# Attention's softmax: the reciprocals of the row sums taken on GpSimd as a power, where VectorE's reciprocal took them

## The chip, the cores and the metric

The kernel runs on one core of a Trainium2 chip. The metric is the time of one execution on the device in microseconds (us), the median of the runs shown. The engines are named as in the profile: PE is TensorE (matrix products; PEld its weight loads), DVE is VectorE, ACT is ScalarE, POOL is GpSimd, SP is SyncE, which here issues the DMAs. Each engine works through its own queue in program order and waits on the others through semaphores.

## What the kernel computes

Sparse attention over 4 batches, 8 heads, 576 positions, 64 features per head, and behind it two dense layers. Only the attention is touched by the change; the rest is cut to one line each.

```python
scores = scale * np.matmul(q, k.transpose(0, 1, 3, 2))
...
mask_local = (rel >= 0) & (rel < stride)
mask_strided = (rel >= 0) & (pos[None, :] % stride == pos[:, None] % stride)
...
scores = scores - np.max(scores, axis=-1, keepdims=True)
attn = np.exp(scores)
attn = attn / (np.sum(attn, axis=-1, keepdims=True) + 1e-09)
return np.matmul(attn, v).astype(np.float32)
...
h = x @ w_in;  x = (h * np.cos(h)) @ w_out          # first layer, 512 -> 2048 -> 512
...
g = x @ w_gate;  return (silu(g) * (x @ w_val)) @ w_out   # second layer, 512 -> 1536 -> 512
```

The first four heads use the local mask (32 keys back), the last four the strided one (each 32nd key).

## The kernel before

The attention stage works on pairs of heads. A unit is one batch and one pair; the 16 units are taken two at a time, a strided one and a local one, and each is cut into three groups (`gs`, line 780). That makes 48 groups, a strided one (tiles `e_s`, `qks`, `pts`) and a local one (`e_l`, `qkl`, `pt`) in turn. A group holds three or four small softmax tiles side by side, 128 rows by 3x96 or 4x54 scores.

The order is written out by hand in one loop (line 816). Step k of it does one part of each of several groups, so that every part of a group lies some steps behind the one before it (`LAGS = (2, 5, 6, 7)`): the scores and the row maxima of group k, the exponentials of group k-1, the sums and the division of group k-2, the transposes of group k-5, the product with the values of group k-6, and the copy out of group k-7.

Who does what for a group: PE makes the scores (L464, L466, L467), the transposes (L499, L503) and the products with v (L521). DVE takes the maxima (`top`, L472) and the sums with the reciprocals (`sums`, L488, and `norm`, L491). POOL scales the maxima (L473) and multiplies the exponentials by the reciprocals (L493, in place in `e_s` or `e_l`). ACT makes the exponentials (L479) and empties PSUM (L510, L534, L543). The sums lie in a small tile `ls`, 128 rows by 3 or 4, of which there are five.

Between these parts the same loop hands out work for the weights of the layers that follow (`pump`, line 854): ACT reads raw weights (L252) and rounds them (L273), DVE takes their maxima (L255, L202), shifts and joins their bits (L259, L263) and makes the remainders (L276). In a step this filling stands in DVE's queue behind the sums and the maxima, and ahead of the reciprocals, since `norm` is called after `pump`.

Behind the attention come the first dense layer (L579 to L581 with L612 to L627), and the second one, which makes up most of the time.

Of the kernel before, what the change touches and what calls it, by code (L numbers as in the profile page):

```python
# [10 lines left out]
F32 = mybir.dt.float32  # L11
# [4 lines left out]
ALU = mybir.AluOpType  # L16
# [65 lines left out]
def build(tc, qk_l, qk_s, v_l, v_s, w_in, w_out, w_gate, w_val, w_out2, fixed, out):  # L82
    nc = tc.nc
    wide = w_in.dtype != F32
    with ExitStack() as ctx:
# [317 lines left out]
        ap = attn.enter_context(tc.tile_pool(name="attn", bufs=2, side="right"))  # L403
# [7 lines left out]
        e_l = [ap.tile([128, 3, LW + 1], F32, name=f"e_l{i}", bufs=1) for i in range(4)]  # L411
        hot = ap.tile([128, 512], BF16, name="hot", bufs=1)
        nc.vector.memset(hot, 1.0)
        v_pair = [ap.tile([128, 2 * SP, 128], F32, name=f"v_pair{i}", bufs=1) for i in range(2)]
        for d in e_s:
            nc.gpsimd.memset(d, 0.0)
# [29 lines left out]
        class Group:  # L446
# [41 lines left out]
                nc.vector.tensor_reduce(out=self.l, in_=self.e[..., 0:self.w + 1], op=ALU.add, axis=AX.X)  # L488

            def norm(self):  # L490
                nc.vector.reciprocal(out=self.l, in_=self.l)  # L491
                e = self.e[..., 0:self.w]
                nc.gpsimd.tensor_tensor(out=e, in0=e, in1=self.l.unsqueeze(len(e.shape) - 1).to_broadcast(list(e.shape)), op=ALU.mult)  # L493

# [875 lines left out]
```

## Time and profile before

| what | us |
|---|---|
| median of three runs | 852.34 |
| lowest and highest of them | 852.09, 852.67 |
| the profiled execution, its own time | 853.48 |
| its span, from the first instruction to the last | 851.7 |
| PE busy in the span | 842.2 |
| DVE busy | 649.6 |
| ACT busy | 519.3 |
| POOL busy | 199.6 |

The span is the part of the profiled execution that the trace shows; 1.8 us of its time lie around it. Busy times are averages over stages with different limits. The attention stage is the first 100 us or so of the span.

### The profile page before, as it was taken

How to read it: one execution, taken by the hardware profiler on the slowest of the kernel's cores; microseconds unless marked ns; L12 is line 12 of the kernel's file. 1: busy time of each engine (PE TensorE's matmuls, PEld its weight loads, DVE VectorE, ACT ScalarE, POOL GpSimd, SP SyncE). 2: the span in 40 equal slices, each digit the busy share in tenths (PEclk: the TensorE clock that was granted, in tenths of full speed). 3: DMA queues.
4: the chain of work that ended last, by engine and by line, in shares of the span. 5: the costliest groups of instructions: out<-in, count | busy, mean ns of one | idle time of the engine just before them, and what ended most of it. 6: DMA issues, size and time to landing. Idle time of an engine off the chain costs nothing.

```text
span 851.7 us, 18335 instructions
## 1 busy us (share of the span) xinstructions
PE 842.2 (99%) x7228; PEld 601.5 (71%) x7228; DVE 649.6 (76%) x1242; ACT 519.3 (61%) x1047; POOL 199.6 (23%) x281
## 2 busy tenths in 40 slices
PE   8999999999999999999999999999999999999998
PEld 5777544444444444566666888888888899999998
DVE  6999988997889878799996388567756765765562
ACT  6899989554656766778885466545445454444440
POOL 3554234111445546422223001000000000000000
PEclk9999999999999999999999999999999999999999
DMA  9998822897557566415356257767767688788894
GB/s 367 408 373 288 275 74 99 291 337 262 184 196 237 198 210 214 170 42 188 115 214 238 78 185 284 253 220 260 237 246 261 222 284 290 278 310 312 318 329 149
DMA packets 53622, 202.23 MB, mean 237 GB/s; under 512 B 5280, under 2 KB 15904, under 8 KB 49696
## 3 DMA queue, kind: packets, MB, share of 16 engines
q1 hardware_dynamic: 53536, 201.06, 66.5%
q8 instruction: 57, 0.93, 0.4%
q14 instruction: 29, 0.24, 0.1%
HBM read 177.05 MB, written 23.99 MB: 236 GB/s over the span
## 4 chain that ended last, share of the span: by engine, by line
PE 84%; DVE 7%; ACT 4%; DMA 2%; issue 1%; POOL 1%; SPq 0%; ACTq 0%; POOLq 0%
PE acc L733 13%; PE bank L579 12%; PE bank L581 12%; PE bank L580 12%; PE acc L581 7%; PE acc L579 7%; PE acc L580 7%; PE bank L464 3%; PE po L521 3%; DMA raw<-w_val 2%; POOL arena L627 1%; PE tp L499 1%; PE bank L466 1%; DVE pw_two L202 1%; PE bank L733 1%
## 5 line engine op out<-in xcount | busy, mean ns | idle before, releaser
L579 PE MATMUL bank<-xs,wi 128*128 128x256 f16 (+3 forms) x780 | 232.6, 298 | 0.8 <-DVE arena L1231 0.7
L581 PE MATMUL bank<-xs,wi 128*128 128x256 f16 (+3 forms) x780 | 232.6, 298 | 0.0
L580 PE MATMUL bank<-xs,wi 128*128 128x256 f16 (+3 forms) x780 | 232.6, 298 | 0.0
L627 POOL TENSOR_TENSOR arena<-tb,arena 128x512 f16<-128x512 f32 (+1 forms) x80 | 89.8, 1123 | 236.1 <-ACT arena L626 197.2
L581 PE MATMUL acc<-arena 128*128 128x512 f16 (+1 forms) x320 | 114.5, 358 | 1.4 <-DVE arena L276 1.4
L579 PE MATMUL acc<-arena 128*128 128x512 f16 (+1 forms) x320 | 114.5, 358 | 0.0
L580 PE MATMUL acc<-arena 128*128 128x512 f16 (+1 forms) x320 | 114.5, 358 | 0.0
L580 PEld LDWEIGHTS <-wi 128*128 128x128 f16 x880 | 86.1, 98 | 35.7 <-issue 1.2
L581 PEld LDWEIGHTS <-wi 128*128 128x128 f16 x880 | 86.1, 98 | 34.8
L579 PEld LDWEIGHTS <-wi 128*128 128x128 f16 x880 | 86.1, 98 | 34.7
L733 PEld LDWEIGHTS <-arena 128*128 128x128 f16 x1080 | 100.7, 98 | 8.2
L717 POOL TENSOR_TENSOR wi<-tb 128x256 f32<-128x256 f32 (+1 forms) x30 | 20.2, 674 | 337.4 <-DVE tb L699 337.4
L1231 DVE TENSOR_TENSOR arena<-bank,cv 128x512 f32<-128x512 f32 (+1 forms) x60 | 37.9, 636 | 66.0 <-PE bank L581 66.0
L702 ACT ACTIVATE arena<-tb 128x256 f16<-128x256 f32 (+3 forms) x59 | 28.7, 486 | 97.0 <-DVE tb L699 88.5
L581 PEld LDWEIGHTS <-arena 128*128 128x128 f16 x600 | 58.7, 98 | 34.6 <-DVE arena L276 1.9
L580 PEld LDWEIGHTS <-arena 128*128 128x128 f16 x600 | 58.7, 98 | 32.5
L579 PEld LDWEIGHTS <-arena 128*128 128x128 f16 x600 | 58.7, 98 | 32.4
L733 PE MATMUL acc<-arena 128*128 128x256 f16 (+1 forms) x684 | 80.2, 266 | 0.0
L626 ACT ACTIVATE arena<-tb 128x512 f16<-128x512 f32 (+1 forms) x80 | 46.6, 583 | 53.1 <-PE acc L581 51.6
L612 ACT ACTIVATE tb<-bank,quarter,c 128x512 int32<-128x512 f32 (+1 forms) x75 | 54.5, 726 | 27.3 <-PE bank L581 18.9
L699 DVE SCALAR_TENSOR_TENSOR tb<-tb,c,arena 128x512 f32<-128x512 f32 (+1 forms) x60 | 41.7, 695 | 34.5 <-ACT tb L694 34.4
L1227 ACT ACTIVATE cv<-bank 128x512 f32<-128x512 f32 (+1 forms) x90 | 49.3, 548 | 29.6 <-PE bank L581 28.6
(147 smaller groups left out, 1713.4 us busy)
## 6 DMA issues: line engine op xcount, KB each, us to landing
wi<-w SPq DMA_DIRECT2D x20, 1792.0 KB, 7.4
arena<-w SPq DMA_DIRECT2D x60, 576.0 KB, 4.9
raw<-w_out SPq DMA_DIRECT2D x56, 512.0 KB, 4.9
arena<-w SPq DMA_DIRECT2D x10, 1792.0 KB, 8.5
raw<-w_gate SPq DMA_DIRECT2D x24, 512.0 KB, 4.3
raw<-w_val SPq DMA_DIRECT2D x24, 512.0 KB, 5.6
w<-arena SPq DMA_DIRECT2D x42, 256.0 KB, 3.3
raw<-w_in SPq DMA_DIRECT2D x16, 512.0 KB, 9.1
```

The source lines that it names most:

```text
L464: nc.tensor.matmul(out=self.sc[r, i, :], lhsT=qk_t[self.i][r, q0:q0 + 64], rhs=qk_t[self.i][r, k0:k0 + w], start=i == 0, stop=False)
L579: nc.tensor.matmul(out=o, lhsT=w[:, 0, c], rhs=x[0], start=first, stop=False, **kw)
L580: nc.tensor.matmul(out=o, lhsT=w[:, 0, c], rhs=x[1], start=False, stop=False, **kw)
L581: nc.tensor.matmul(out=o, lhsT=w[:, 1, c], rhs=x[0], start=False, stop=last, **kw)
L612: nc.scalar.activation(out=c["w"].bitcast(I32), in_=c["ph"], func=AF.Identity, scale=turn[c["blk"]], bias=quarter)
L626: nc.scalar.activation(out=g[:, 0, 0:n], in_=w, func=AF.Copy)
L627: nc.gpsimd.tensor_tensor(out=g[:, 1, 0:n], in0=w, in1=g[:, 0, 0:n], op=ALU.subtract)
L699: nc.vector.scalar_tensor_tensor(out=t, in0=t, scalar=s_g[c["blk"]], in1=c["C"][m][:, 1, 0:c["n"]], op0=ALU.mult, op1=ALU.mult)
L702: nc.scalar.activation(out=to, in_=src, func=AF.Copy, scale=2.0 ** -11)
L733: nc.tensor.matmul(out=o[:, c], lhsT=w[:, 256 * i + 128 * c:256 * i + 128 * c + 128], rhs=unit(u)[:, x:x + h], start=j == i == 0 and c == ...
L1227: nc.scalar.activation(out=t, in_=src, func=AF.Copy)
L1231: nc.vector.tensor_tensor(out=c["C"][m][:, :, h * right:h * right + h], in0=p, in1=t, op=ALU.add)
```

## The change

A tile `minus` of 128 by 4 is filled with -1 once, at the start, by DVE. In `norm`, DVE's reciprocal of `ls` goes, and POOL raises each sum to the power of the matching element of `minus`, in place in `ls`; the multiplication of the exponentials by `ls` follows it on POOL as before. For a strided group of three tiles the power now covers three columns, where the reciprocal covered all four.

```diff
         hot = ap.tile([128, 512], BF16, name="hot", bufs=1)
         nc.vector.memset(hot, 1.0)
+        minus = ap.tile([128, 4], F32, name="minus", bufs=1)
+        nc.vector.memset(minus, -1.0)
...
             def norm(self):
-                nc.vector.reciprocal(out=self.l, in_=self.l)
+                l = self.ls[:, 0:self.n]
+                nc.gpsimd.tensor_tensor(out=l, in0=l, in1=minus[:, 0:self.n], op=ALU.pow)
                 e = self.e[..., 0:self.w]
                 nc.gpsimd.tensor_tensor(out=e, in0=e, in1=self.l.unsqueeze(len(e.shape) - 1).to_broadcast(list(e.shape)), op=ALU.mult)
```

POOL's queue at the first groups of the stage (`mx` are the maxima, `ls` the sums, `e_s_98` and `e_l_102` the exponentials of the first strided and local group), before:

```order
L473 TENSOR_SCALAR mx<-mx 128x4
L493 TENSOR_TENSOR e_s_98<-e_s_98,ls 128x2x2x54
L473 TENSOR_SCALAR mx<-mx 128x3
L493 TENSOR_TENSOR e_l_102<-e_l_102,ls 128x3x96
L473 TENSOR_SCALAR mx<-mx 128x3
```

and of the change, where lines 473 and 493 have become 475 and 496:

```order
L475 TENSOR_SCALAR mx<-mx 128x4
L494 TENSOR_TENSOR ls<-ls,minus 128x4
L496 TENSOR_TENSOR e_s_98<-e_s_98,ls 128x2x2x54
L475 TENSOR_SCALAR mx<-mx 128x3
L494 TENSOR_TENSOR ls<-ls,minus 128x3
L496 TENSOR_TENSOR e_l_102<-e_l_102,ls 128x3x96
L475 TENSOR_SCALAR mx<-mx 128x3
```

Each step now has one instruction more on POOL, between the scaling of the maxima of group k and the multiplication of group k-2. The multiplication waits for POOL's own power where it waited for DVE.

DVE's queue at two steps in the middle of the stage (`wi` and `raw` are the weights of the filling), before:

```order
L259 TENSOR_SCALAR wi<-wi 128x512
L491 RECIPROCAL ls<-ls 128x4
L488 TENSOR_REDUCE ls<-e_l_102 128x3
L472 TENSOR_REDUCE mx<-bank 128x3
L263 SCALAR_TENSOR_TENSOR wi<-raw,wi 128x512
L255 TENSOR_REDUCE pw_in<-raw 128x1
L491 RECIPROCAL ls<-ls 128x3
L488 TENSOR_REDUCE ls<-e_s_99 128x4
```

and of the change, with 488 now 490 and 472 now 474:

```order
L259 TENSOR_SCALAR wi<-wi 128x512
L490 TENSOR_REDUCE ls<-e_l_102 128x3
L474 TENSOR_REDUCE mx<-bank 128x3
L263 SCALAR_TENSOR_TENSOR wi<-raw,wi 128x512
L255 TENSOR_REDUCE pw_in<-raw 128x1
L490 TENSOR_REDUCE ls<-e_s_99 128x4
```

The reciprocals, which stood behind the filling of their step, are gone, and nothing else of DVE's order has moved. PE, ACT and SP keep their orders.

## Rows read from the trace of the kernel before

**Rows 1.** The page: the span, and busy time, share and instructions of engines.
```profile
span 851.7 us, 18335 instructions
PE 842.2 (99%) x7228; PEld 601.5 (71%) x7228; DVE 649.6 (76%) x1242; ACT 519.3 (61%) x1047; POOL 199.6 (23%) x281
```

**Rows 2.** Busy time in stretches (start:end, length, busy by engine, clock, DMA, GB/s).
```profile
20.00:90.00 70.00, 70.00 (x1173) 50.34 (x1171) 66.95 (x192) 65.50 (x249) 35.43 (x76) 1.00 0.93 350
...
200.00:220.00 20.00, 18.26 (x88) 8.14 (x87) 14.09 (x31) 9.57 (x16) 3.48 (x3) 1.00 0.41 155
```

**Rows 3.** The chain that ended last (start, length, work): scores of three-tile strided groups.
```profile
20.50 0.49 PE bank L464 x12
...
31.65 0.49 PE bank L464 x12
...
87.44 0.49 PE bank L464 x12
```

**Rows 4.** PE's waits from 10 to 110 us, all of them.
```profile
PE po L521 <- ACT pt L510: 0.3, 1, 0.3
```

**Rows 5.** POOL's groups by shape: count, busy us, mean ns, idle before and releasers.
```profile
L493 POOL TENSOR_TENSOR e_l<-e_l,ls 128x288 f32<-128x288 f32 x24 | 16.0, 667 | 17.7 <-DVE ls L491 12.5 <-ACT xy L534 2.3 <-ACT pt L510 2.1
L493 POOL TENSOR_TENSOR e_s<-e_s,ls 128x216 f32<-128x216 f32 x24 | 13.2, 549 | 19.2 <-DVE ls L491 8.6 <-ACT pts L510 3.7 <-PE bank L467 2.3
...
L473 POOL TENSOR_SCALAR mx<-mx 128x3 f32<-128x3 f32 x32 | 10.0, 311 | 5.1 <-DVE ls L491 2.2 <-DVE mx L472 1.7
...
L473 POOL TENSOR_SCALAR mx<-mx 128x4 f32<-128x4 f32 x16 | 5.4, 336 | 8.0 <-DVE mx L472 7.0 <-DVE ls L491 0.9
...
L417 POOL MEMSET e_s<- 128x4 f32 x4 | 0.4, 102 | 0.2
```

**Rows 6.** Line 491's instructions: ns min/median/max, first and last start.
```profile
L491 DVE RECIPROCAL ls<-ls x48: 159/167/172, 10.1 to 95.4; 128x4 f32<-128x4 f32 x24, 128x3 f32<-128x3 f32 x24
```

**Rows 7.** Timeline of DVE, start and length, from 7.0 and from 41.9 us.
```profile
7.83 0.38 DVE L472 TENSOR_REDUCE mx<-bank 128x4 f32<-128x216 f32 x1 [3.01 <-PE bank L467]
...
41.99 0.17 DVE L491 RECIPROCAL ls<-ls 128x4 f32<-128x4 f32 x1
42.08 0.42 DVE L488 TENSOR_REDUCE ls<-e_l 128x3 f32<-128x291 f32 x1
42.42 0.45 DVE L472 TENSOR_REDUCE mx<-bank 128x3 f32<-128x288 f32 x1
42.79 0.68 DVE L263 SCALAR_TENSOR_TENSOR wi<-raw,wi 128x512 int32<-128x512 int32 x1
```

**Rows 8.** Timeline of POOL from 41.0 us, and ACT's next exponentials.
```profile
41.24 0.19 POOL L473 TENSOR_SCALAR mx<-mx 128x4 f32<-128x4 f32 x1 [0.32 <-DVE mx L472]
42.34 0.55 POOL L493 TENSOR_TENSOR e_s<-e_s,ls 128x216 f32<-128x216 f32 x1 [0.91 <-PE po L521]
42.96 0.56 POOL L473 TENSOR_SCALAR mx<-mx 128x3 f32<-128x3 f32 x1
...
42.77 0.94 ACT L479 ACTIVATE e_s<-bank,mx 128x54 f32<-128x54 f32 x4
```

**Rows 9.** Timeline of POOL at the start: a memset that waits for POOL's own.
```profile
0.90 0.31 POOL L416 MEMSET e_s<- 128x256 f32 x1
1.27 0.10 POOL L417 MEMSET e_s<- 128x4 f32 x1
```

**Rows 10.** Lines 259, 263 and 276 until 100 us: ns min/median/max, first and last start.
```profile
L259 DVE TENSOR_SCALAR wi<-wi x16: 409/418/679, 18.6 to 74.0; 128x512 int32<-128x512 int32 x16
...
L263 DVE SCALAR_TENSOR_TENSOR wi<-raw,wi x16: 679/692/889, 19.0 to 74.7; 128x512 int32<-128x512 int32 x16
...
L276 DVE SCALAR_TENSOR_TENSOR wi<-wi,s x11: 735/751/1175, 79.2 to 99.6; 128x512 f16<-128x512 f32 x11
```

**Rows 11.** Timeline of POOL and DVE at 125 us, behind the attention stage.
```profile
125.42 1.16 POOL L627 TENSOR_TENSOR arena<-tb,arena 128x512 f16<-128x512 f32 x1 [1.78 <-ACT arena L626]
...
125.79 1.33 DVE L263 SCALAR_TENSOR_TENSOR cv<-raw,cv 128x512 int32<-128x512 int32 x1
```

## The prediction

> **What bounds the kernel now.** I read the page first: PE is busy for 842.2 of 851.7 us, DVE for 649.6, POOL for only 199.6 [rows 1]. The shares of the whole say little about a change that touches the first 100 us, so the next view was the busy time of the stretch from 20 to 90 us, the steady part of the attention stage. There PE is busy for all 70 us, DVE for 66.95, ACT for 65.50 and POOL for 35.43 [rows 2]. Three engines are nearly full and the fourth is half full.
>
> Which of the three sets the pace shows in the chain of waits and in PE's own waits. In the chain the stage is PE's work end to end. The scores of a strided group of three tiles (0.49 us) come round once in six steps, at 20.50, 31.65 and so on to 87.44: seven of them, with six intervals of 11.15 or 11.16 us in the mean [rows 3]. A step lasts 11.15 / 6 = 1.858 us, and it does so whatever the filling in it is. From 10 to 110 us PE has a single wait, of 0.3 us [rows 4]. So PE paces the stage by its own instructions; DVE and ACT fit under it with 4 to 6 per cent to spare, and the reader should not take DVE's 96 per cent for the bound.
>
> POOL's 50 per cent are one scaling of the maxima and one multiplication in each step. Over 48 steps the scalings take 10.0 + 5.4 = 15.4 us and the multiplications 16.0 + 13.2 = 29.2 us [rows 5], together 0.93 us in a step. So POOL has 1.86 - 0.93 = 0.93 us free in a step. The rows put most of that idle time down to waiting for the reciprocal, line 491 [rows 5].
>
> **What is removed.** 48 reciprocals of 0.167 us leave DVE [rows 6]. What one holds up there is less: the sums behind it start 42.08 - 41.99 = 0.09 us after it [rows 7], so DVE's queue is lighter by 48 x 0.09 = 4.3 us. I count this as nothing, because PE paces these steps and does not wait for DVE. The multiplication's wait for DVE goes too. A reciprocal stands behind the filling of its step, while the sums stand before it; the power can start when the sums and the scaling of the next maxima are done, in the row at 41.24 + 0.19 = 41.43, where the multiplication starts at 42.34 [rows 8]. These 0.9 us are the same free time seen from the other side, and the power spends it.
>
> **What is added on DVE.** One memset of 128 by 4. POOL's memset of that size took 0.10 us [rows 5]; DVE sits idle for 3.01 us before the first maxima [rows 7], which covers it. Without that cover it would cost 0.1 us.
>
> **What is added on POOL.** 48 powers, and a wait of the multiplication for its own engine. The wait has a row: the memset at 1.27 waits for the one that ends at 0.90 + 0.31 = 1.21, so 0.06 us [rows 9].
>
> No row shows a power. From below, the nearest row is the scaling of the maxima, of the same engine and size, 0.19 us where nothing delays it [rows 8]; it does two multiplications. A memset of the size takes 0.102 us [rows 5], so reading and two arithmetic operations on four columns cost 0.09 us over the bare instruction. A power needs a logarithm, a product and an exponential. I take six such pairs of operations beyond the scaling, 0.19 + 6 x 0.093 = 0.75 us; as the upper bound I take fifteen, 0.19 + 15 x 0.093 = 1.6 us. The low end is 0.19 us itself. Six and fifteen are chosen, not read; it is the weakest point of the working. A mean of 0.75 us lies nearer to the scaling than to the multiplication of 512 columns by line 627, 1.16 us [rows 11].
>
> **How much of the free time the power can use.** Not all 0.93 us. The scaling takes 0.19 us alone, but 15.4 / 48 = 0.32 us in the mean [rows 5]: the one at 42.96 lasts 0.56 us and ends with DVE's L263, which runs from 42.79 to 43.47 [rows 7, 8]. It stands just where DVE begins its filling. The multiplication escapes this today, since it starts behind the filling (its reciprocal is last there). With the change both the power and the multiplication follow the scaling at once, in the middle of the filling. I give each of them the scaling's mean delay, 0.32 - 0.195 = 0.125 us, 0.25 together. What is left for the power is 0.93 - 0.06 - 0.25 = 0.62 us.
>
> **The sum.** Power 0.75 less 0.62 is 0.13 us a step by which POOL, not PE, then paces the stage; over 48 steps 6.2 us. What is late next: POOL's scaling of the maxima, which stands in the same queue behind the multiplication, with the exponentials waiting for it. From its end at 41.43 to the exponentials at 42.77 there are 1.3 us of reserve [rows 8], used up in the first ten steps; after that ACT, then the banks of the scores and the transposes on PE, wait in turn. I let this reserve stand against the longer first steps. I count on nothing behind the stage to give it back. Against the profiled execution that is 853.48 + 6.2 = 859.7 us; that execution lies 1.1 us above the median of 852.34, and the runs' median is what is forecast: 858.5 us.
>
> **The rules beside it.** That DVE and POOL hold each other up is a row: L263 at 125.79 takes 1.33 us beside a POOL multiplication that runs from 125.42 to 126.58, and its median is 0.69 [rows 10, 11]. The Trainium skill, "SBUF — State Buffer", section "SBUF: two separate sides", says that DVE instructions with two SBUF inputs or in a two-port mode share a port pair with GpSimd under an exclusive lock held for the whole instruction. By that rule the trace agrees, and the longer POOL's power is, the longer DVE is shut out; the third rival below is what this would do. The Trainium skill, "GPSIMD Engine Reference", section 4.1, advises VectorE for elementwise work and calls GpSimd about twice as slow with two inputs. By that factor alone the power would take an estimated 2 x 0.167 = 0.33 us, and the sum would be no change; no run here shows that the factor holds for a power, which is no simple operation.
>
> **The rivals.**
>
> *The power is cheap: no change.* It decides from 0.62 us downward. Then POOL's free time covers it, PE goes on pacing the stage at 1.858 us a step, and the time stays at 852.3 us (851 to 854). For it speaks that the scaling with its two operations costs only 0.19 us; against it that a power is many operations.
>
> *The power is dear: much slower.* Above the upper bound, if the engine takes it in a slow form. Each us beyond 0.62 costs 48 us: at 1.6 us 899, at 2.6 us 947.
>
> *DVE becomes the bound.* DVE has 70 - 66.95 = 3.05 us free in 70 [rows 2], 0.08 us a step, and gains 0.09. In the stage it has 16 + 16 + 11 = 43 instructions of the kind that POOL shuts out [rows 10], 0.9 a step. If each meets the power and the multiplication (0.75 + 0.61) and waits half of them, that is 0.9 x 0.68 = 0.61 us, 0.44 more than is free, and over 48 steps 21 us: 873 us. Against it: instructions that wait for each other also spread out, and not each meets one.
>
> *DVE's relief pays: faster.* DVE holds the path later, and the one stretch where PE then loses time is 200 to 220 us, 20 - 18.26 = 1.74 us [rows 2]. If the 4.3 us of relief arrived there, the time would be 850.6. Against it: PE ends the attention stage when it did, and the program ties DVE's order to PE's.
>
> **How the numbers follow.** The forecast, POOL pacing the stage with a power of 0.62 to 1.6 us, gets 0.42; the cheap power 0.34; the dear one 0.14; DVE as the bound 0.05; the relief 0.05. The forecast's own range is 853 to 899. The range to hold it 8 times in 10 runs from 850.5 (the relief) to 890 (a power of 1.4 us), and leaves out the dear power and the upper end of the forecast. About 0.2 per cent (1.7 us) is what a measurement of this kernel can tell from no change. Faster: 0.05, the relief. Same: 0.34 and 0.02 of the forecast, powers just over 0.62. Slower: the rest, 0.40 + 0.14 + 0.05 = 0.59.
>
> **What would show it.** The new line's instructions on POOL show the power's length; the whole rests on that. If POOL paces the stage, its busy time from 20 to 90 us is above 60 of 70 us, the multiplication is released by POOL itself and never by DVE, the six-step interval grows from 11.15 to about 11.9 us, and PE shows waits for ACT or POOL there. If the power is cheap, the interval stays at 11.15 and POOL's idle time is before the scaling, released by DVE's maxima. Behind the stage everything should be shifted and otherwise unchanged. The prediction is wrong if the power lies outside 0.62 to 1.4 us, if POOL's two instructions wait for DVE much more or less than 0.25 us, or if the lengthened L259, L263 and L276 hold DVE up beyond what it has free.

## The result and the profile after

The change made the kernel slower: 852.50 us before, 857.43 us after, medians of six runs each, 4.9 us apart. The ratio of the runs is 1.0052 with a 95% interval of 1.0042 to 1.0063, which is 3.6 to 5.4 us. The forecast was 858.5 us. The profiled execution took 857.72 us, with a span of 855.8 where it was 851.7.

On the page, POOL now works nearly without a break until the attention stage ends. Engines, and POOL's busy tenths in 40 slices of the span:

```profile
PE 844.3 (99%) x7228; PEld 601.9 (70%) x7228; DVE 648.2 (76%) x1195; ACT 519.0 (61%) x1047; POOL 244.3 (29%) x329
...
POOL 6999734211355536522323100000000000000000
```

The stretches of [rows 2], now with POOL full and PE, DVE and ACT each short of what they did before:

```profile
20.00:90.00 70.00, 68.80 (x1145) 49.15 (x1146) 63.70 (x149) 63.14 (x239) 66.82 (x109) 1.00 0.90 337
...
200.00:220.00 20.00, 18.81 (x91) 8.40 (x90) 14.18 (x32) 8.65 (x14) 2.70 (x3) 1.00 0.55 213
```

POOL's 66.82 of 70 us are a different 95 per cent from DVE's 96 in [rows 2]: DVE's left PE alone, and POOL's do not. POOL's groups by shape say why. Where [rows 5] had 17.7 and 19.2 us of idle time before the multiplications (now L496), there are 1.9 and 1.9, and before the powers (L494) none:

```profile
L494 POOL TENSOR_TENSOR ls<-ls,minus 128x3 f32<-128x3 f32 x32 | 29.2, 914 | 0.0
L496 POOL TENSOR_TENSOR e_l<-e_l,ls 128x288 f32<-128x288 f32 x24 | 16.8, 701 | 1.9
L494 POOL TENSOR_TENSOR ls<-ls,minus 128x4 f32<-128x4 f32 x16 | 16.3, 1016 | 0.0
L496 POOL TENSOR_TENSOR e_s<-e_s,ls 128x216 f32<-128x216 f32 x24 | 14.2, 593 | 1.9
...
L475 POOL TENSOR_SCALAR mx<-mx 128x3 f32<-128x3 f32 x32 | 9.0, 281 | 1.1 <-DVE mx L474 0.8
...
L475 POOL TENSOR_SCALAR mx<-mx 128x4 f32<-128x4 f32 x16 | 5.4, 340 | 6.3 <-DVE mx L474 6.3
```

A power takes (29.2 + 16.3) / 48 = 0.948 us in the mean, a multiplication 31.0 / 48 = 0.646, a scaling 14.4 / 48 = 0.300: 1.894 us of records in a step of which PE needs 1.858. PE's waits from 10 to 120 us, where [rows 4] had a single one:

```profile
PE tp L506 <- POOL e_s L496: 2.3, 5, 0.8
PE tp L502 <- POOL e_l L496: 0.8, 3, 0.3
PE po L524 <- ACT pt L513: 0.3, 1, 0.3
```

Short waits do not show in this list: 14 of the 48 groups of transposes begin 0.05 us after the end of their multiplication, eight of them listed here, where in the kernel before the least distance is 0.18 us.

The first of the waits stand at the start of the stage. In POOL's timeline the first power delays the first multiplication, which began at 10.45 before, to 11.50; the last multiplication began at 95.69 before and begins at 101.27 now. Before:

```profile
10.45 0.55 POOL L493 TENSOR_TENSOR e_s<-e_s,ls 128x216 f32<-128x216 f32 x1
...
95.69 0.67 POOL L493 TENSOR_TENSOR e_l<-e_l,ls 128x288 f32<-128x288 f32 x1 [0.78 <-DVE ls L491]
```

Now:

```profile
10.40 1.03 POOL L494 TENSOR_TENSOR ls<-ls,minus 128x4 f32<-128x4 f32 x1
11.50 0.55 POOL L496 TENSOR_TENSOR e_s<-e_s,ls 128x216 f32<-128x216 f32 x1
...
101.27 0.67 POOL L496 TENSOR_TENSOR e_l<-e_l,ls 128x288 f32<-128x288 f32 x1
```

From 11.50 to 101.27 there are 47 intervals of 1.910 us. That is POOL's pace, and over the middle of the stage it is PE's too, in the mean. PE's scores of three-tile strided groups [rows 3] started at 20.43 and 87.37 before, and the last product with the values at 99.16:

```profile
20.43 0.56 PE L464 MATMUL bank<-qks 64*64 64x54 f32 x12
...
87.37 0.56 PE L464 MATMUL bank<-qks 64*64 64x54 f32 x12
...
99.16 0.57 PE L521 MATMUL po<-pt,vl 96*64 96x64 f32 x12
```

Now they start at 21.91 and 90.75, with six intervals between them, singly 11.18 to 12.07 us and in the mean 68.84 / 36 = 1.912 us a step, and the last product at 103.86:

```profile
21.91 0.56 PE L466 MATMUL bank<-qks 64*64 64x54 f32 x12
...
90.75 0.56 PE L466 MATMUL bank<-qks 64*64 64x54 f32 x12
...
103.86 0.57 PE L524 MATMUL po<-pt,vl 96*64 96x64 f32 x12
```

So PE is 21.91 - 20.43 = 1.5 us late after two turns of the stage (the scores that [rows 3] show from 20.50 begin at 20.43 in the timeline), 90.75 - 87.37 = 3.4 at the eighth, and 103.86 - 99.16 = 4.7 at the end: 1.5 by the start, 1.9 by the pace, 1.3 by the end, where the last transposes wait for POOL three times more (0.27, 0.27 and 0.47 us). POOL's starts give the same 4.7 us in another way. Before, the 47 intervals took (95.69 - 10.45) / 47 = 1.814 us in the mean, less than PE's middle step, since PE's first steps hold no transposes and products yet (the scores of strided groups, two steps apart, begin at 8.69, 10.55 and 12.82, and from there every 3.8 us). So POOL begins 1.05 us late, needs 47 x 0.096 = 4.5 us more until its last multiplication, and 0.9 us of that are taken from the distance between this one's end and the last product, 2.80 us before and 1.92 now. Behind the stage 0.55 us come back from 200 to 220 us (18.81 busy where it was 18.26), and 4.1 us of span remain.

### The profile page after: what moved, and what is told of

Same layout as the page of the kernel before. It is cut to its first block, busy times and chain, and to the rows that moved or that the text cites. A ratio compares the mean times of both kernels' runs of the same rounds, so it can differ in the third digit from the quotient of the medians.

```text
span 855.8 us, 18339 instructions
## 1 busy us (share of the span) xinstructions
PE 844.3 (99%) x7228; PEld 601.9 (70%) x7228; DVE 648.2 (76%) x1195; ACT 519.0 (61%) x1047; POOL 244.3 (29%) x329
## 4 chain that ended last, share of the span: by engine, by line
PE 74%; DVE 9%; ACT 7%; POOL 6%; issue 2%; DMA 2%; POOLq 0%; SPq 0%; ACTq 0%
PE acc L736 13%; PE bank L582 12%; PE bank L583 12%; PE bank L584 12%; PE acc L584 7%; PE acc L582 7%; PE acc L583 7%; DMA raw<-w_val 2%; POOL ls L494 2%; POOL arena L630 1%; ACT tb L615 1%; DVE pw_two L202 1%; PE bank L736 1%; POOL e_l L496 1%; ACT e_l L481 1%
```

## The experiments

The theory: POOL's time sets the pace, whatever it spends it on. The rivals: the multiplication merely comes later than its transposes can bear; DVE, shut out by POOL or freed of the reciprocals, decides. Each kernel is given with its median, its ratio to the kernel before that ran beside it, and the start of the last product with the values (99.16 us before), which shows how much of the loss lies in the stage.

| kernel | median us | over before | ratio | last product |
|---|---|---|---|---|
| the change | 857.43 | +4.9 | 1.0052 (1.0042 to 1.0063) | +4.7 |
| e2_beside | 857.40 | +4.6 | 1.0057 (1.0043 to 1.0070) | +5.2 |
| e4_double | 896.03 | +43.1 | 1.0508 (1.0494 to 1.0521) | +43.6 |
| e11_noscale | 853.94 | +1.0 | 1.0011 (1.0002 to 1.0020) | +1.1 |
| e7_column | 853.09 | +0.2 | 1.0002 (0.9993 to 1.0011) | +0.3 |
| e3_cheap | 853.03 | +0.1 | 1.0000 (0.9991 to 1.0009) | +0.5 |
| e1_swap | 856.07 | +3.2 | 1.0040 (1.0027 to 1.0052) | +3.4 |
| e12_vscale | 857.89 | +5.1 | 1.0060 (1.0046 to 1.0073) | +5.4 |
| e5_stream | 861.74 | +8.9 | 1.0105 (1.0091 to 1.0119) | +9.5 |
| e6_late | 862.99 | +10.2 | 1.0122 (1.0108 to 1.0135) | +9.7 |
| e9_lag | 855.84 | +2.9 | 1.0037 (1.0024 to 1.0049) | +1.5 |
| e8_power_lag | 859.06 | +6.1 | 1.0071 (1.0059 to 1.0084) | +4.7 |
| e10_early | 867.74 | +14.8 | 1.0154 (1.0127 to 1.0182) | +16.3 |

**A power that nobody waits for (e2_beside).** The kernel before keeps its reciprocal, and POOL takes a power of constants ahead of each multiplication.

```diff
                 nc.vector.reciprocal(out=self.l, in_=self.l)
+                nc.gpsimd.tensor_tensor(out=spare, in0=three, in1=minus, op=ALU.pow)
```

> The kernel before with VectorE's reciprocal, and on POOL ahead of each multiplication a power of a constant tile of 128 by 4 into a spare tile that nothing reads. Theory (POOL's time): 0.30 for the scaling, 1.02 for the power of four columns, 0.65 for the multiplication, 1.97 us a step against 1.86, so 48 x 0.11 = 5 us above before: 857 us (855 to 860), although no result depends on the power. Rival (the longer way from the sums to the multiplication, or its wait for POOL's own power): both are gone here, so 852.5 us.

857.40 us, as the theory said. A loss of the change's size is there without its dependence, so it is POOL's time that costs. Its parts differ a little: this power covers four columns in every step and takes 1.053 us against 0.948, but no instruction needs its result, and the multiplications, from 11.33 to 102.21, come every 1.934 us where the change has 1.910.

**Two powers (e4_double).** The change, with a second one of constants behind the first.

```diff
                 nc.gpsimd.tensor_tensor(out=l, in0=l, in1=minus[:, 0:self.n], op=ALU.pow)
+                nc.gpsimd.tensor_tensor(out=spare[:, 0:self.n], in0=three[:, 0:self.n], in1=minus[:, 0:self.n], op=ALU.pow)
```

> The changed kernel with a second power behind the first, of a constant tile into a spare one that nothing reads. Theory (POOL's work runs without a gap from the first power to the last multiplication): 48 x 0.95 = 45.6 us more, 903 us (898 to 908). Rival (only what the multiplication waits for in the first and last groups counts): the queue is as long for the others, so they would lose little, and the time stays below 875 us.

896.03 us, 38.6 over the change: POOL's time costs step by step, somewhat less than expected (903, at least 898). POOL's timeline in this kernel shows why:

```profile
51.90 0.85 POOL L497 TENSOR_TENSOR ls<-ls,minus 128x3 f32<-128x3 f32 x1
52.73 0.84 POOL L498 TENSOR_TENSOR spare<-three,minus 128x3 f32<-128x3 f32 x1
53.55 0.66 POOL L500 TENSOR_TENSOR e_l<-e_l,ls 128x288 f32<-128x288 f32 x1
```

The multiplication's wait for its own power is gone under the second one, and records of neighbours overlap by 0.02 us. From the first power to the multiplication it is 1.65 us here, where the change has 0.94 (46.67 to 47.61, shown below), so this second power adds 0.71 us. Over all steps it adds 38.6 / 48 = 0.80 us in the mean, where its records take 0.92 and the expectation took 0.95. POOL is not quite without a break either, since from 10 to 150 us it waits for DVE's maxima:

```profile
POOL mx L478 <- DVE mx L477: 3.1, 6, 0.8
```

**POOL's time given back (e11_noscale).** The change without the scaling of the maxima, which leaves a power of 0.97 us in the mean.

```diff
-                nc.gpsimd.tensor_scalar(out=m, in0=m, scalar1=SCALE, scalar2=1.0, op0=ALU.mult, op1=ALU.mult)
```

> The changed kernel without the scaling of the maxima (the exponentials take the unscaled maximum, so their values are off), on POOL or anywhere else. Theory (POOL's unbroken work of 1.91 us a step): 0.95 + 0.65 + 0.06 = 1.66 us, under TensorE's 1.86; POOL sits idle again before its powers, the interval in the middle is 11.15 us, and the time 853 us (852 to 854), with what is left at the start, where the first multiplication still ends late. Rival (the power shuts VectorE out, which the swap of the scaling to VectorE left open at 856.1 us): VectorE has no more work than with the change and the power is as long, so 856 us or above. Then the 856.1 us of the swap were VectorE's own added work.

853.94 us, and POOL has idle time again, with PE full:

```profile
20.00:90.00 70.00, 70.00 (x1175) 50.40 (x1175) 65.70 (x154) 65.19 (x248) 60.26 (x75) 1.00 0.93 348
```

With 0.3 us a step less on POOL the interval is 11.15 us again from 21.16 on, which is 0.7 us later than before (20.43). The full power then costs 1.0 us in all, 0.7 of it at the start of the stage, and the last product is 1.1 us late. So the two parts of the loss come apart: the start, and the pace.

**A cheap instruction in the power's place.** A multiplication by -1 (e3_cheap), or a power of the first column alone (e7_column), with the same order on every engine.

```diff
-                nc.gpsimd.tensor_tensor(out=l, in0=l, in1=minus[:, 0:self.n], op=ALU.pow)
+                nc.gpsimd.tensor_tensor(out=l, in0=l, in1=minus[:, 0:self.n], op=ALU.mult)
```

> The changed kernel with a multiplication of the sums by minus one in place of the power, so that the rows are not divided by their sums; it should take some 0.2 us. Theory (the length of the power is the whole cost): 852.5 us (851 to 853.5), since VectorE's lighter queue buys nothing. Rival (VectorE's relief pays): 850.6 us or below, and TensorE is busier than 18.3 us from 200 to 220 us. Rival (POOL's wait for itself, or the new order of its queue, costs by itself): above 854.

```diff
-                l = self.ls[:, 0:self.n]
-                nc.gpsimd.tensor_tensor(out=l, in0=l, in1=minus[:, 0:self.n], op=ALU.pow)
+                l = self.ls[:, 0:1]
+                nc.gpsimd.tensor_tensor(out=l, in0=l, in1=minus[:, 0:1], op=ALU.pow)
```

> The changed kernel with the power on one column of each group alone, so that the other tiles are not divided by their sums. A power of three columns took 0.85 us and one of four 1.02, 0.16 a column, so some 0.53 us here. First theory (POOL's time per step): 0.30 + 0.53 + 0.65 + 0.06 = 1.54 us fit under 1.86, so 852.5 us (851.5 to 853.5). Second theory (the end of the multiplication): the first transposes come 0.4 us later than before, the rest fits, 853 us. If the time of a power doesn't go by columns, 857 us as with the change.

Neither can be told from the kernel before: 853.03 and 853.09 us. The first shows that the move itself, DVE's relief and the new wait are worth less than 1 us either way; the second that 0.615 us on POOL still fit:

```profile
L494 POOL TENSOR_TENSOR ls<-ls,minus 128x1 f32<-128x1 f32 x48 | 29.5, 615 | 0.0
```

**The scaling moved to DVE**, with the power on POOL (e1_swap), and alone in the kernel before (e12_vscale).

```diff
-                nc.gpsimd.tensor_scalar(out=m, in0=m, scalar1=SCALE, scalar2=1.0, op0=ALU.mult, op1=ALU.mult)
+                nc.vector.tensor_scalar(out=m, in0=m, scalar1=SCALE, scalar2=1.0, op0=ALU.mult, op1=ALU.mult)
```

> The power stays on POOL, and the scaling of the maxima goes from POOL to VectorE in its place. Theory (POOL's time per step sets the pace): POOL has left 0.95 for the power, 0.65 for the multiplication and 0.06 for its own wait, 1.66 us a step and so less than TensorE's 1.86; the six-step interval goes back to 11.15 us and the time to that of before, 852.5 us (851 to 854). Rival (the power on POOL shuts VectorE out of the memory port): the power and the multiplication are still there and VectorE has one small instruction more, so the time stays at 857 us or above.

> The kernel before, reciprocal on VectorE, with the scaling of the maxima moved from POOL to VectorE; no power anywhere. If the 856.1 us of the swap were VectorE's own added work (0.17 us a step for the scaling, where 0.08 us were free), the time is 856 us or above here too, since the reciprocal's 0.09 us are not even taken off. If they were the power's (its length at the start and the end of the stage), the time is 852.5 to 853.5 us.

The first missed: 856.07 us, where POOL, with time to spare, should have made it 852.5. The second kernel says what went wrong, since it has no power at all and is as slow. Busy time in the first kernel, and in the second:

```profile
20.00:90.00 70.00, 68.64 (x1147) 49.20 (x1145) 67.23 (x184) 63.15 (x240) 57.69 (x73) 1.00 0.92 340
```

```profile
20.00:90.00 70.00, 66.36 (x1110) 47.50 (x1106) 67.35 (x213) 60.55 (x231) 21.22 (x35) 1.00 0.90 333
```

POOL is idle for 12 and for 49 us there, and PE is short by 1.4 and 3.6 us all the same. DVE, at 67.2 to 67.4 of 70, is where most of the loss is then: in the second kernel POOL's multiplications wait for DVE's reciprocals for 33.9 us from 20 to 90 us (20.3 in the kernel before), and near 60 us PE waits 1.0 us in the first and 1.1 in the second for DVE's line 134, a part of the filling. DVE is a second bound right under PE's, and has no room for 48 more instructions. In the first kernel the power's start is in the loss as well: the scores that began at 20.43 begin at 21.34 there, 0.9 us late, and at 20.75 in the second, which has no power.

**Another load on POOL (e5_stream).** The kernel before with a multiplication of 128 by 384 on POOL ahead of each of its own.

```diff
                 nc.vector.reciprocal(out=self.l, in_=self.l)
+                nc.gpsimd.tensor_tensor(out=spare, in0=three, in1=three, op=ALU.mult)
```

> As the power beside the reciprocal, but the idle instruction on POOL is a multiplication of 128 by 384, which takes about as long as the power (some 1.0 us, from the 0.73 us of 128x256 and the 0.59 us of 128x192 on line 717) and reads and writes memory all the while. Theory that only POOL's time counts: 857 us as with the power (855 to 860). Rival (what POOL does with the memory port counts): VectorE's lines 259, 263 and 276 wait for it, are above 0.9 us in the mean, and the time is 865 us or more; and the power, which took as long, was then cheaper than its length for VectorE.

861.74 us: it costs nearly twice what e2_beside's power costs, with a shorter instruction and with POOL not full (58.25 of 70). The rows of the added instruction and of DVE's line 263, from 10 to 106 and 101 us, here and in e2_beside:

```profile
L495 POOL TENSOR_TENSOR spare<-three 128x384 f32<-128x384 f32 x48 | 41.1, 857 | 0.0
...
L263 DVE SCALAR_TENSOR_TENSOR wi<-raw,wi 128x512 int32<-128x512 int32 x16 | 16.8, 1049 | 0.3
```

```profile
L497 POOL TENSOR_TENSOR spare<-three,minus 128x4 f32<-128x4 f32 x48 | 50.5, 1053 | 0.0
...
L263 DVE SCALAR_TENSOR_TENSOR wi<-raw,wi 128x512 int32<-128x512 int32 x16 | 13.8, 862 | 0.3
```

Line 263 goes from a mean of 0.715 us in the kernel before to 1.049 here and to 0.862 in e2_beside. In e2_beside it is not the power that lengthens it. The eight of line 263 that begin beside a power take 0.68 to 0.72 us; the other eight, 0.89 to 1.20, begin while one of POOL's own multiplications runs, which now come later. Two of each engine, POOL first:

```profile
44.68 1.01 POOL L497 TENSOR_TENSOR spare<-three,minus 128x4 f32<-128x4 f32 x1
...
47.59 0.67 POOL L499 TENSOR_TENSOR e_l<-e_l,ls 128x288 f32<-128x288 f32 x1
```

```profile
45.38 0.68 DVE L263 SCALAR_TENSOR_TENSOR wi<-raw,wi 128x512 int32<-128x512 int32 x1
...
47.60 1.20 DVE L263 SCALAR_TENSOR_TENSOR wi<-raw,wi 128x512 int32<-128x512 int32 x1
```

So line 263, with its two inputs, pays for the columns that POOL moves, not for POOL's time.

**A later multiplication, and more room for it.** The kernel before with `norm` one step later (e6_late); the kernel before (e9_lag) and the change (e8_power_lag) with one step more between multiplication and transposes.

```diff
-            if group(LAGS[0]):
-                group(LAGS[0]).norm()
+            if group(LAGS[0] + 1):
+                group(LAGS[0] + 1).norm()
```

> The kernel before, with reciprocal and multiplication of each group one step later in the program. Theory (POOL's time): nothing is longer, the transposes come two steps behind the multiplication in place of three, and the time stays at 852.5 us (851 to 854). Rival (a later end of the multiplication is what TensorE waits for at the transposes): the multiplication ends 1.86 us later in every step, more than the power adds, so 856 us or above.

```diff
-LAGS = (2, 5, 6, 7)
+LAGS = (2, 6, 7, 8)
```

> Control: the kernel before with the same later lags (2, 6, 7, 8). Both theories: nothing waited there, so no gain; one more step at the end of the stage costs up to 1 us. 853 us (852 to 855).

> The changed kernel with transposes, values and copy out one step later in the program (lags 2, 6, 7, 8). First theory (POOL's 1.91 us a step against TensorE's 1.86 paces the stage): nothing changes for POOL, so the loss of 4.9 us against the same lags without the change stays. Second theory (the multiplication ends too late for the transposes three steps on, for which there is 1.0 us of reserve; at the start, where they wait for 0.78 and 0.33 us, and at the end): the extra step gives 1.86 us more, TensorE's first waits for POOL go, and the loss against the control falls to the 2 us or so by which POOL's steps are longer in the middle.

The first missed widely: 862.99 us. The delay is not free, and PE's waits from 10 to 120 us name the place, with POOL busy for only 30.49 of 70 us:

```profile
PE tp L503 <- POOL e_s L493: 4.6, 9, 0.9
PE tp L499 <- POOL e_l L493: 3.1, 4, 1.5
```

In the kernel before, the multiplication that starts at 42.34 [rows 8] ends at 42.89 and its transposes begin at 43.97, so about 1.0 us is all that this multiplication can be late, where a step is 1.86. The reserve differs from group to group, from 0.18 to 3.06 us. I had not looked at it. So lateness alone can cost too, and the second pair was to weigh it for the change. The step more costs 2.9 us by itself, where 1 at most was expected (1.5 of it in the stage), and the power on top of it 859.06 - 855.84 = 3.2 us: between the 4.9 of the theory and the 2 of the rival, and so undecided in size. PE's waits for POOL fall from 3.1 to 0.4 us, but PE waits 3.6 us for ACT's copies (`pt`, `pts`), of which 1.9 are there in e9_lag as well, and POOL stays full at 66.94 of 70 us. What the pace takes can't be had back by room; some of the loss at the ends may be.

**An earlier reciprocal (e10_early).** The kernel before, with DVE's reciprocal right behind the sums, ahead of the maxima and the filling.

```diff
+                nc.vector.reciprocal(out=self.l, in_=self.l)
...
             def norm(self):
-                nc.vector.reciprocal(out=self.l, in_=self.l)
```

> The kernel before with VectorE's reciprocal right behind the sums and ahead of the maxima and the filling, so that the multiplication can start some 0.9 us earlier in a step. Theory (TensorE paces that stage and nothing waits for the multiplication): 852.5 us (851.5 to 853.5). Rival (the multiplications' ends are already felt in the first and last groups): 851 us or below.

The widest miss: 867.74 us (861.90 to 870.42). The multiplication leaves its place behind the filling and runs beside it, as POOL's row and DVE's in this kernel show:

```profile
42.23 0.66 POOL L493 TENSOR_TENSOR e_l<-e_l,ls 128x288 f32<-128x288 f32 x1
```

```profile
42.24 1.20 DVE L263 SCALAR_TENSOR_TENSOR wi<-raw,wi 128x512 int32<-128x512 int32 x1
```

Line 263 takes 0.928 us in the mean, where it took 0.715. DVE falls behind, PE waits 1.73 us for it at 60 us, and then another thing sets in, in the column ahead of the last two:

```profile
60.00:65.00 5.00, 3.27 (x40) 2.43 (x38) 4.19 (x17) 3.15 (x13) 1.74 (x6) 0.64 0.76 211
65.00:70.00 5.00, 5.00 (x53) 3.45 (x49) 3.50 (x9) 3.96 (x13) 2.19 (x3) 0.50 0.92 364
...
80.00:85.00 5.00, 5.00 (x54) 3.58 (x55) 3.70 (x8) 2.11 (x8) 2.00 (x4) 0.50 0.69 241
85.00:90.00 5.00, 5.00 (x64) 3.58 (x65) 2.79 (x9) 2.68 (x10) 0.87 (x3) 0.63 0.37 128
90.00:95.00 5.00, 5.00 (x80) 3.48 (x82) 4.41 (x16) 3.57 (x13) 2.29 (x6) 1.00 0.41 134
```

The granted clock falls to 0.50, 1.2 GHz, and stays there for four stretches of five us. PE's work lost to it can be estimated from these rows as busy time by missing clock: 3.27 x 0.36 + 20 x 0.50 + 5.00 x 0.37 = 13 us of the 16.3 by which the stage ends late. The six runs differ in the same way: 861.90 and 862.53 us at a mean granted clock of 0.996 and 0.994, and 867.66 to 870.42 at 0.982 to 0.988. So most of the loss in the profiled execution is the clock's by this estimate, and the rest the waits'; no run was made to take the two apart.

## Why the prediction was right, and where its terms were off

**What bounds the kernel.** Right. PE paced the stage; with POOL fuller than a step of PE, POOL does. The six-step interval grew to 11.47 us in the mean (68.84 / 6), POOL is busy for 66.82 us, above the 60 that were named, and the multiplication is released by POOL's own power and never by DVE. e2_beside and e11_noscale show the cause from both sides: POOL's time without the dependence costs as much, and the dependence with less time on POOL costs 1 us.

**The power, 0.75 us.** Too low: 0.948 us in the mean. The bounds of 0.19 and 1.6 held it, and the count of six operations had no better ground than it claimed; no run shows what POOL does inside a power. What it missed is the columns: the shortest powers take 0.54 us with one column (e7_column), 0.85 with three and 1.02 with four, so about 0.16 us a column over 0.38. The Trainium skill, "GPSIMD Engine Reference", section 4.1, gives its factor of about two for adds, multiplications and maxima; taken for the power it would have given an estimated 0.33 us and no change. The trace shows that it does not carry over to a power, at 5.7 times the 0.167 us of the reciprocal [rows 6].

**DVE's delay of POOL, 0.25 us.** Too high, by what the prediction itself named as a sign of being wrong, and this nearly cancels the error of the power. Against undisturbed records (0.85 and 1.02; 0.667 and 0.548) the power lost 0.04 us in the mean, the multiplication 0.04, and the scaling lost 0.02 less than before (0.30 where it was 0.32). Half of the power's loss lies in two of the 48, of 1.39 and 1.30 us, which begin when a line 263 or 276 has just begun. DVE was not held up by the power for long either. In the middle of the stage POOL's power and then DVE's two instructions:

```profile
46.67 0.86 POOL L494 TENSOR_TENSOR ls<-ls,minus 128x3 f32<-128x3 f32 x1
47.61 0.79 POOL L496 TENSOR_TENSOR e_l<-e_l,ls 128x288 f32<-128x288 f32 x1
```

```profile
46.72 0.42 DVE L259 TENSOR_SCALAR wi<-wi 128x512 int32<-128x512 int32 x1
47.18 0.69 DVE L263 SCALAR_TENSOR_TENSOR wi<-raw,wi 128x512 int32<-128x512 int32 x1
```

Both take what they take alone [rows 10], while the power runs until 47.53. The rule of the Trainium skill, "SBUF — State Buffer", section "SBUF: two separate sides", that the pair of ports is held for the whole instruction, would have kept line 263 out until then; it comes near for the multiplication of e10_early (42.23 to 42.89, line 263 from 42.24 with 1.20 us, 0.51 more than alone), and does not hold for the power.

**The free time and the sum.** The 0.62 us that the power could use were too few. POOL's pace is 1.910 us, 0.05 over PE's 1.858, so a power of about 0.948 - 0.05 = 0.90 us would just have fitted (worked out; the runs show only that 0.615 fits and 0.95 does not). The records sum to 1.894 with 0.08 us of the multiplication's own wait (47.53 to 47.61; 0.06 forecast), and neighbours overlap by some 0.03 us where nothing waits. So the excess was 0.05 us a step and not 0.13, 2.5 us over 48 steps and not 6.2.

**The reserve at the start.** This step failed. The scaling's 1.3 us were to stand against the longer first steps, so that only the pace would cost. The path that was tight is another: multiplication to transposes. In the kernel before the first transposes come only 0.21 us behind the end of their multiplication (10.45 + 0.55, to 11.21). The first power delays the first multiplication by 1.05 us at once, and the first transposes wait 0.78 and the next 0.33 us:

```profile
11.21 0.38 PE L503 MATMUL tp<-fix,e_s 128*128 128x128 f32 x2
```

```profile
12.10 0.44 PE L506 MATMUL tp<-fix,e_s 128*128 128x128 f32 x2 [0.78 <-POOL e_s L496]
```

Of the 4.7 us by which the stage ends late, 2.5 are the pace if 0.05 us is taken for all 48 steps (1.9 of them are seen, from 21.91 to 90.75), and 2.2 are what the power adds at the start and at the end, where PE's steps are shorter than the 1.858 us of the sum. e11_noscale, where the pace is PE's, loses 1.0 us. The sum had 6.2 of pace and nothing for the ends. So the mechanism was right by itself. That the size came within 1.1 us is luck: the power too short and the delay too long nearly cancel, and the pace too dear stands against the ends left out.

**DVE's relief, nothing.** Right: e3_cheap has it, with 64.37 us of DVE in the 70 where it was 66.95, and is no faster. **The rivals.** The cheap power fell by the power's length, and e3_cheap and e7_column are what it would have looked like. DVE as the bound did not come: DVE has less to do, 63.70 us; but e12_vscale, e5_stream and e10_early show how near it is, by 48 small instructions, by a stream on POOL, and by a multiplication beside the filling. The dear power did not come, at 0.948 us.

## What to carry to other kernels

An idle engine's share is room only per step: add up what the step would hold there, and compare it with the step of the engine that paces. Moving a small operation to GpSimd frees nothing if VectorE did not pace, and a power there takes 5.7 times as long as VectorE's reciprocal, and goes by the column. Before an instruction is moved earlier or later, look at what it will run beside and at its distance to the consumer, since here moving the multiplication earlier (14.8 us) or later (10.2 us) cost more than the power did.

## What was not expected of the hardware

The power's time goes by the column, 0.16 us each over 0.38. A power of 0.86 us leaves VectorE's line 263, which has two inputs, at 0.69 us beside it, where a multiplication of 288 columns that begins just ahead makes it 1.20. And a wait of 1.7 us on TensorE in a full stage, with shorter ones before it, was followed by some 27 us at a granted clock of 0.50 (e10_early; 3.6 + 20 + 3.7 from its rows from 60 to 90 us, of which those at 0.64 and 0.63 are mixed); in e4_double, where PE also waits, the mean granted clock from 20 to 90 us is 0.72:

```profile
20.00:90.00 70.00, 64.92 (x816) 45.09 (x814) 45.38 (x102) 46.91 (x169) 67.68 (x103) 0.72 0.69 247
```

There it costs little that the runs show, since POOL sets the pace: POOL's waits for DVE's maxima, which in turn wait for PE's scores, come to 3.1 us. What TensorE must do to keep its clock, no run here was made to tell: e5_stream waits 8.0 us for POOL, DVE and ACT, in small pieces, and e6_late up to 1.5 us at once, and both keep 1.00.
